# Gate chunk in three passes, late weight parts on VectorE, four tap sums on TensorE, mu in the first load, no table of shifts

## Chip, cores and metric

The kernel runs on one core of a Trainium2 chip. The metric is device time in microseconds (us). PE is TensorE's matmul engine and PEld its weight load, DVE is VectorE, ACT is ScalarE, POOL is GpSimd, SP is SyncE, which issues the kernel's DMAs.

## The reference

Three layers act on two batches of 4160 tokens with 192 channels, all in fp32.

```python
# 1: a convolution of 7 taps whose weights are a softmax per token and head (8 heads of 24 channels)
w = softmax(weight_gen, over the 7 taps)
x[b, s, h] = sum over k of w[b, s, k, h] * x_pad[b, s + k, h]
# 2: x_prev is x of the token before
xk = mu_k * x + (1 - mu_k) * x_prev
xr = mu_r * x + (1 - mu_r) * x_prev
x = sigmoid(xr @ w_r) * (relu(xk @ w_k) ** 2 @ w_v)       # 192 -> 1024 -> 192
# 3: h has 1024 channels, conv_w has 3 taps per channel
h = relu(x @ w_in)
x = (h * sigmoid(conv3(h, conv_w))) @ w_out
```

Each weight arrives as 64-bit floats; the kernel makes fp32 of it from two 32-bit words.

## The kernel before

Tokens are cut into 10 tiles (`SIZES`): two of 238, seven of 476 and one of 352 tokens, each for both batches. Channels stand on partitions: a 192-channel tensor is one block of 128 partitions and one of 64. To keep fp32 accuracy with fast fp32r matmuls, an operand is split into a high part and a low remainder, and a product is hi x hi, lo x hi and hi x lo. A 128-channel input takes three such passes; a 64-channel input has its high and its low part on the two halves of the partitions and takes two. So one product of 192 channels is five passes (`passes_in`, line 660).

Per tile the work is this. `attention` (530) does layer 1 with tokens on partitions, in 2, 4 or 3 slots of 128 tokens per batch. For a slot, `token` multiplies a window of 7 x 192 elements by the softmax weights into one of two `prod` buffers, and sums the 7 taps by three adds, all on POOL. For tile 0 alone the sum is made by seven fp32 matmuls with the identity (`total`) and copied out by ScalarE. `mixing` (574) transposes the sums on PE, mixes neighbouring tokens with mu and splits the result; the remainders are made on POOL, the 64-channel block is brought to its place by DMAs (`xB`). `moe1` (682) makes one chunk of 128 hidden channels of layer 2: five passes, relu, square, split, and five more passes into the accumulators `am` (128 channels) and `ar` (64 channels, high and low weight beside each other). There are 8 chunks. `gate_r` (664) makes the sigmoid gate in two chunks of five passes: channels 0 to 127, and channels 128 to 191, which stand twice in the weights (`wrA`, `wrB`, columns 128 to 255) so that the gate of the 64 channels lies on both halves of the partitions. `mix_out` (818) multiplies gate and accumulators and splits the product into `x2`; slice 3 of it holds the 64 channels' high part on the lower partitions and their remainder on the upper ones. `moe2` (854) is layer 3, again 8 chunks: five passes, relu, three taps, sigmoid, product, split (`c7` makes the high part on ScalarE; `c8` the remainder, on POOL from tile 7 on), five passes. `store` (913) adds the halves and writes out. Tiles 0 and 1 use the `_half` versions.

The weights come in 16 chunks (`prepare`, 478; the last of them are taken up between planner times 6 and 18: `w_in`, `w_out`, `conv_w`). `narrow` (399) makes fp32 of one: ScalarE scales the upper word, VectorE shifts and masks it and scales the lower word by the exponent, and PE adds the two in PSUM, with one fp32 matmul (identity) and one fp32r matmul. `split` (423) copies the high part on ScalarE, subtracts it on PE, and copies the remainder on ScalarE.

The order is made by a planner. Every step is put into `plan` with a time (`at`, 367), where one chunk is 1 and a tile 16, so tile i starts at 16 i. The steps become instructions, and `schedule` (168) is a list scheduler: with a cost per instruction (`cost`, 138) it picks, on the engine that is free first, the ready instruction with the lowest time. The order that results is issued as the program order of each engine's queue, SyncE's DMAs among them. `ORDER` (40) shifts the times of 393 of the 2983 plan items; its indices run from 11 to 1084, which are the loads, the softmax and tiles 0 to 4.

```python
    def at(t, fn, hold=0.0):
        plan.append((t + ORDER.get(len(plan), 0.0), len(plan), fn, hold))
```

Of the kernel before, what the change touches and what calls it, by code (L numbers as in the profile page):

```python
# [96 lines left out]
class Program:
# [986 lines left out]
```

## Time and profile before

| | |
|---|---|
| median of 3 runs | 736.1 us (734.06 to 736.75) |
| execution profiled | 739.15 us |
| its span, first to last instruction | 737.3 us |
| granted TensorE clock, mean | 0.989 of full |
| busy: PE, DVE, ACT, POOL | 706.5, 580.1, 646.6, 537.8 us |
| DMA | 44.58 MB, mean 60 GB/s |

Busy time is the union of an engine's instructions. A matmul's shown end is modelled and overlaps the next one, so what a pass costs in a run of passes is read from the length of the run, not from one pass. An idle stretch in brackets names what ended it.

### The profile page before, as it was taken

Reading aid. Unit: us, or ns where it says so; the run is one execution under the profiler, and the core shown is the slowest. Engines: PE = TensorE matmul, PEld = TensorE weight load, DVE = VectorE, ACT = ScalarE, POOL = GpSimd, SP = SyncE. Lnnn points to the kernel's source line nnn. Section 1 sums busy time; section 2 is a strip of 40 time slices with the busy share of each in tenths; the row PEclk is TensorE's granted clock in tenths of the full one; section 3 lists DMA queues with packets and bytes.
Section 4 is the critical chain, followed back from the end, with each engine's and each line's share of the span. In section 5 each row is a group of like instructions: output and inputs, shape, how many; then the busy total and the mean of one; then the engine's idle time right before and its main releaser. Section 6 shows DMA issues by size and latency. Waiting matters only on the chain.

```text
span 737.3 us, 10455 instructions
## 1 busy us (share of the span) xinstructions
PE 706.5 (96%) x3475; PEld 607.1 (82%) x3475; DVE 580.1 (79%) x959; ACT 646.6 (88%) x1340; POOL 537.8 (73%) x392
## 2 busy tenths in 40 slices
PE   4899988999999999999999999999999999999996
PEld 4687966888778888888888888888888888899995
DVE  5865968887998988787878787978796758686775
ACT  2788859999989999899989898989899989899986
POOL 1998997898999899999999999999022323242333
PEclk9899999999999999999999999999999999999999
DMA  8667112101211320231112202210002000200000
GB/s 271 196 198 228 56 54 54 39 35 59 68 39 55 88 75 1 73 80 48 54 58 57 87 1 69 74 48 1 21 15 59 1 20 7 55 0 21 1 21 29
DMA packets 18149, 44.58 MB, mean 60 GB/s; under 512 B 2864, under 2 KB 13616, under 8 KB 17968
## 3 DMA queue, kind: packets, MB, share of 16 engines
q1 hardware_dynamic: 18096, 43.93, 19.7%
q8 instruction: 27, 0.44, 0.3%
q14 instruction: 26, 0.21, 0.1%
HBM read 27.40 MB, written 6.39 MB: 46 GB/s over the span
## 4 chain that ended last, share of the span: by engine, by line
PE 80%; POOL 8%; ACT 6%; issue 3%; DVE 2%; DMA 1%; POOLq 0%; SPq 0%; ACTq 0%; DVEq 0%
PE pa L237 25%; PE pc L237 18%; PE bm L237 12%; PE am L237 11%; PE br L237 8%; PE ar L237 7%; POOL prod L237 5%; ACT pa L237 1%; DMA mu<-in_mu_dram 1%; ACT pc L237 1%; POOL s L237 1%; ACT L237 1%; DVE stage L237 1%; POOL xA L237 1%; POOL tok L237 0%
## 5 line engine op out<-in xcount | busy, mean ns | idle before, releaser
L237 DVE SCALAR_TENSOR_TENSOR pc<-h,cw,pc 128x476 f32<-128x476 f32 (+1 forms) x276 | 194.3, 705 | 40.4 <-ACT pc L237 37.4
L237 POOL TENSOR_TENSOR prod<-rows,sw 128x1344 f32<-128x1344 f32 x68 | 210.4, 3096 | 16.1 <-PE pa L237 15.2
L237 ACT ACTIVATE pa<-pa 128x476 f32<-128x476 f32 (+2 forms) x284 | 153.1, 540 | 31.7 <-PE pa L237 28.5
L237 POOL TENSOR_TENSOR prod<-prod 128x576 f32<-128x576 f32 (+1 forms) x132 | 161.5, 1223 | 9.3
L237 PE MATMUL bm<-g,wo 128*128 128x476 f32 (+1 forms) x411 | 133.1, 378 | 3.3 <-ACT g L237 2.8
L237 PE MATMUL am<-s,wv 128*128 128x476 f32 (+2 forms) x464 | 135.1, 359 | 0.0
L237 PE MATMUL pa<-xA,wkA 128*128 128x476 f32 (+2 forms) x450 | 117.6, 366 | 2.0 <-DVE s L237 1.5
L237 POOL TENSOR_TENSOR g<-stage,g 128x476 fp32r<-128x476 f32 (+1 forms) x41 | 47.5, 1158 | 97.5 <-ACT g L237 93.6
L237 PE MATMUL pc<-x,wiA 128*128 128x478 f32 (+1 forms) x414 | 113.2, 379 | 0.7 <-ACT x L237 0.6
L237 PE MATMUL ar<-s,wv 128*128 128x476 f32 (+2 forms) x336 | 106.5, 355 | 3.6 <-ACT s L237 3.6
L237 DVE TENSOR_TENSOR s<-pa,s 128x476 fp32r<-128x476 f32 (+1 forms) x139 | 88.1, 634 | 18.7 <-ACT s L237 18.2
L237 PE MATMUL br<-g,wo 128*128 128x476 f32 (+1 forms) x274 | 102.5, 375 | 0.0
L237 PEld LDWEIGHTS pa<-xA,wkA 128*128 128x128 f32 x450 | 79.7, 189 | 19.1 <-DVE s L237 5.5
L237 ACT ACTIVATE pc<-h,cw 128x476 f32<-128x476 f32 (+1 forms) x138 | 92.4, 670 | 1.2
L237 PEld LDWEIGHTS am<-s,wv 128*128 128x128 f32 x464 | 82.1, 189 | 11.2 <-ACT s L237 0.9
L237 DVE TENSOR_TENSOR pc<-h,pc 128x476 f32<-128x476 f32 x96 | 62.8, 654 | 33.7 <-ACT pc L237 33.5
L237 PEld LDWEIGHTS bm<-g,wo 128*128 128x128 f32 x411 | 75.9, 188 | 15.4 <-ACT g L237 4.3
L237 ACT ACTIVATE pc<-pc 128x476 f32<-128x476 f32 (+1 forms) x148 | 81.2, 548 | 8.2 <-DVE pc L237 6.5
L237 PEld LDWEIGHTS pc<-x,wiA 128*128 128x128 f32 x414 | 76.2, 190 | 12.7 <-DVE g L237 2.0
L237 ACT ACTIVATE h<-pc 128x478 f32<-128x478 f32 (+1 forms) x138 | 79.0, 573 | 8.4 <-PE pc L237 7.5
L237 PE MATMUL pa<-xB,wkB 128*128 128x476 f32 (+2 forms) x300 | 84.5, 361 | 0.6 <-DMA xB<-mk 0.6
L237 PE MATMUL pc<-x,wiB 128*128 128x478 f32 (+1 forms) x276 | 82.4, 377 | 0.0
(161 smaller groups left out, 1190.0 us busy)
## 6 DMA issues: line engine op xcount, KB each, us to landing
rows<-in_x_dram SPq DMA_DIRECT2D x14, 960.0 KB, 4.8
xB<-rm SPq DMA_DIRECT2D x28, 119.0 KB, 2.3
rows<-in_x_dram SPq DMA_DIRECT2D x4, 768.0 KB, 6.5
xB<-mk SPq DMA_DIRECT2D x16, 119.0 KB, 2.3
rows<-in_x_dram SPq DMA_DIRECT2D x2, 864.0 KB, 4.3
out_dram<-stage SPq DMA_DIRECT2D x7, 238.0 KB, 2.0
out_dram<-om SPq DMA_DIRECT2D x7, 238.0 KB, 2.0
stage<-in_moe_w_v_dram SPq DMA_DIRECT2D x4, 384.0 KB, 6.0
```

What stands on the lines that cost most here:

```text
L237: getattr(self.real[eng], method)(*a, **k)
```

## The change

The second gate chunk uses weights that have the high part in columns 128 to 191 and the low part in 192 to 255. Three passes give hi x and lo x on the two halves of the partitions; ScalarE copies the upper half down, VectorE adds it, and after the sigmoid a DMA copies the result to the upper half. Two DMAs (`swap`) put the low parts there after tiles 0 and 1, whose `gate_half` uses the old layout. `mix_out` makes its second copy of the 64 channels by a DMA in place of a ScalarE copy.

The weight chunks 8, 9, 10 and 12 to 15 (`w_in`, `w_out`) get mode 2: no matmul, and the remainder comes from a subtraction and an addition on VectorE. For slots 2 and 3 of both batches of tile 2, `total` sums the taps on PE. `mu` comes as four more columns of the first load of softmax weights. In the last batch of the last tile, POOL makes the high part of chunks 0 to 4 and VectorE the remainders of chunks 6 and 7, and the last two passes swap places. The last softmax load has a later time and hold, one of the softmax's additions goes from VectorE to ScalarE for the later tiles, the planner's price for a DMA out of SBUF goes from 0.45 to 0.58, and `ORDER` goes.

```diff
+HIGH = range(5)
+LOWS = {(NTILE - 1, NB - 1, k) for k in range(6, NF)}
+SUMS = {(2, 0, 2), (2, 0, 3), (2, 1, 2), (2, 1, 3)}
+MODES = [0, 0, 0, 0, 0, 0, 0, 0, 2, 2, 2, 0, 2, 2, 2, 2, 2]
-ORDER = {
...
         if method == "dma_start":
-            return 0.45, 0.0
+            return 0.58 if src == ["SBUF"] else 0.45, 0.0
...
     def at(t, fn, hold=0.0):
-        plan.append((t + ORDER.get(len(plan), 0.0), len(plan), fn, hold))
+        plan.append((t, len(plan), fn, hold))
...
     def narrow(st, n):
...
+        ACT.activation(px, f(hi), ACTF.Prelu, scale=2.0 ** -112, alpha=-(2.0 ** 32))
+        if mode[0] == 0:
...
         DVE.tensor_scalar(x, x, 3, None, op0=ALU.logical_shift_left)
         DVE.tensor_scalar(y, x, 0xFF800000, None, op0=ALU.bitwise_and)
+        zr = wz_r()[:, :n] if mode[0] == 1 else py
+        DVE.scalar_tensor_tensor(out=zr, in0=lo, scalar=2.0 ** -52, in1=py, op0=ALU.mult, op1=ALU.mult)
+        return Parts(px, wl_r()[:, :n], zr)
...
     def split(dst_hi, dst_lo, x):
+        if isinstance(x, Parts):
+            px, zl, zr = x.aps
+            ACT.copy(dst_hi, px)
...
+                DVE.tensor_tensor(zl, px, f(dst_hi), op=ALU.subtract)
+                DVE.tensor_tensor(dst_lo, zr, f(zl), op=ALU.add)
+            return
...
     def softmax_load(j, wg, t, hold=0.0):
-        w = sm[j][0]
+        w = both[:, (4 + KH * soft_at[j]) * (j > 0):4 + KH * soft_at[j + 1]]
...
         def s5():
-            DVE.tensor_scalar(z, z, 1e-9, None, op0=ALU.add)
+            if bank is None:
+                ACT.activation(z, z, ACTF.Copy, bias=1e-9)
...
-            if i < 1:
+            if i < 1 or (i, b, l) in SUMS:
                 def total():
...
                     for k in range(KS):
                         PE.matmul(z, lhsT=ident, rhs=y[:, k], start=(k == 0), stop=(k == KS - 1))
...
+                    if i:
+                        ACT.copy(x[:, l], z)
+                        return
...
     def gate_r(i, b, k, t):
         def go():
...
+            if k:
+                mm(p[:, :N], [(wrA[:, 0, 128:256], A[:, 0, :N]), (wrA[:, 0, 128:256], A[:, 1, :N]), (wrB[:, 0, 128:256], B[:, :N])])
+            else:
+                mm(p[:, :N], passes_in(wrA, wrB, A, B, slice(0, 128), N))
+        def fold():
+            a = attt_r()[0:64, :N]
+            ACT.copy(a, st["p"][64:128, :N])
+            DVE.tensor_tensor(st["p"][0:64, :N], st["p"][0:64, :N], a, op=ALU.add)
         def sg():
...
-            ACT.activation(r[:, :N], st["p"][:, :N], ACTF.Sigmoid)
+            ACT.activation(r[h, :N], st["p"][h, :N], ACTF.Sigmoid)
+            if k:
+                SP.dma_start(out=r[64:128, :N], in_=r[0:64, :N])
+        h = slice(0, 64 if k else 128)
         at(t, go)
+        if k:
+            at(t + 0.2, fold)
+        at(t + (0.6 if k else 0.3), sg)
...
         def a1():
-            ACT.copy(X[0:64, 3, c], r[0:64, :N])
             ACT.copy(X[:, 2, c], r[:, :N])
+            SP.dma_start(out=f(X[0:64, 3, c]), in_=f(X[0:64, 2, c]))
...
         def c7():
...
+            if (i, b) == (NTILE - 1, NB - 1) and fi in HIGH:
+                POOL.tensor_copy(g[:, 0, :N], st["q"][:, :N])
+            else:
+                ACT.copy(g[:, 0, :N], st["q"][:, :N])
         def c8():
...
-            (POOL if i >= ALONE else DVE).tensor_tensor(...)
+            (POOL if i >= ALONE and (i, b, fi) not in LOWS else DVE).tensor_tensor(...)
...
     def consts():
-        SP.dma_start(out=mu, in_=mus)
         DVE.tensor_scalar(onemu, mu, -1.0, 1.0, op0=ALU.mult, op1=ALU.add)
...
-    softmax_load(3, wg_rest[:, (slots[1] + slots[2]) * KH:], 18.2, 50.0)
+    softmax_load(3, wg_rest[:, (slots[1] + slots[2]) * KH:], 20.5, 60.0)
...
+    def swap():
+        for W in (wrA, wrB):
+            SP.dma_start(out=f(W[:, 0, DM:256]), in_=f(W[:, 1, 128:DM]))
+    at(30.5, swap)
```

## Rows read from the trace of the kernel before

**Rows 1.** Windows: length; busy us (count) of PE, PEld, DVE, ACT, POOL; clock; DMA

```profile
0.00:60.00 60.00, 46.36 (x247) 38.04 (x248) 41.66 (x83) 39.34 (x103) 39.92 (x34) 0.94 0.71 219
60.00:120.00 60.00, 50.92 (x325) 43.41 (x324) 45.82 (x75) 46.02 (x101) 53.28 (x40) 0.97 0.34 106
280.00:700.00 420.00, 419.91 (x2004) 364.04 (x2003) 328.07 (x527) 384.74 (x780) 282.95 (x205) 1.00 0.13 37
700.00:737.30 37.30, 31.16 (x176) 28.12 (x174) 25.45 (x50) 28.39 (x67) 13.33 (x15) 0.97 0.08 25
```

**Rows 2.** Chain of waits in order of time, 10 to 125: start us, us, what

```profile
66.05 3.01 POOL prod L237
69.13 1.43 POOL prod L237
...
70.62 1.03 POOL prod L237
71.71 0.59 POOL tok L237
...
105.16 2.38 POOL xA L237 x2
```

**Rows 3.** Windows of PE alone: busy us (instructions), clock, DMA share, GB/s

```profile
90.00:95.00 5.00, 3.01 (x23) 1.00 0.01 3
95.00:100.00 5.00, 4.83 (x24) 0.66 0.01 2
110.00:115.00 5.00, 3.70 (x23) 1.00 0.08 18
115.00:120.00 5.00, 2.82 (x13) 1.00 0.79 177
120.00:125.00 5.00, 5.00 (x20) 0.66 0.00 0
```

**Rows 4.** Chain of waits, runs of passes of 476 and of 352 columns

```profile
445.05 1.08 PE pc L237 x5
...
691.47 1.62 PE pa L237 x10
```

**Rows 5.** Timeline around tile 5's mix_out: start us, us, engine, operation, out<-in

```profile
388.36 0.57 ACT L237 CAST x<-ar 64x476 fp32r<-64x476 f32 x1
...
390.32 0.65 DVE L237 TENSOR_TENSOR x<-ar,x 64x476 fp32r<-64x476 f32 x1
...
392.25 0.59 PE L237 MATMUL pc<-x,wiB 128*128 128x478 f32 x2
```

**Rows 6.** DMA issues: count, KB each, median us from issue to landing

```profile
xB<-rm SPq DMA_DIRECT2D x28, 119.0 KB, 2.3
```

**Rows 7.** Waits of SyncE's queue: us in total, times, longest us

```profile
SPq L237 <- POOL prod L237: 199.4, 16, 27.2
```

**Rows 8.** Groups of PE by form, 46.5 to 82: busy us, mean ns | idle before

```profile
L237 PE MATMUL bm<-stage,ident 128*128 128x512 f32 x4 | 2.0, 593 | 0.0
...
L237 PE MATMUL bm<-stage,ident 128*128 128x384 f32 x4 | 1.6, 485 | 0.0
```

**Rows 9.** Timeline of the start, 0 to 24

```profile
0.73 0.20 POOL L237 MEMSET ident<- 128x128 f32 x1 [0.29 <-POOLq L1073]
...
1.01 0.29 POOL L237 TENSOR_SCALAR_AFFINE_SELECT ident<-ident 128x128 f32<-128x128 f32 x1
...
8.43 0.17 DVE L237 TENSOR_SCALAR onemu<-mu 128x4 f32<-128x4 f32 x1 [2.58 <-DMA mu<-in_mu_dram]
8.51 3.03 DVE L237 TENSOR_TENSOR prod<-rows,sw 128x1344 f32<-128x1344 f32 x2
...
20.33 2.51 PE L237 MATMUL pc<-prod,ident 128*128 128x192 f32 x14 [0.61 <-DVE am L237]
```

**Rows 10.** Groups by form, 700 to 737.3

```profile
L237 POOL TENSOR_TENSOR g<-stage,g 128x354 fp32r<-128x354 f32 x8 | 7.6, 950 | 15.3 <-ACT g L237 15.3
...
L237 ACT CAST g<-stage 128x354 fp32r<-128x354 f32 x7 | 3.4, 483 | 0.9 <-DVE stage L237 0.9
```

More of the change, by code (lines that the diff above doesn't have):

```diff
@@ L38 @@
 SPARE = 20
-ORDER = {
[49 rows of a table removed]
-}
 def f(ap):
@@ L251, in conv_moe_kernel @@
 @with_exitstack
-def conv_moe_kernel(ctx: ExitStack, tc: tile.TileContext, xp, wg_first, wg_rest, mus, w_k, w_v, w_r, w_in, conv_w, w_out, out):
+def conv_moe_kernel(ctx: ExitStack, tc: tile.TileContext, xp, wg_first, wg_rest, w_k, w_v, w_r, w_in, conv_w, w_out, out):
     nc = tc.nc
@@ L285, in __call__ @@
             return self.tiles[(self.n - 1) % len(self.tiles)]
-    mu = new("mu", [128, 4])
     onemu = new("onemu", [128, 4])
@@ L311, in conv_moe_kernel @@
     wz_r = Ring([t.rearrange("p a b -> p (a b)") for t in g_r.tiles[:2]])
+    wl_r = Ring([t.rearrange("p a b -> p (a b)") for t in g_r.tiles[2:]])
     rows_r = ring("rows", 2, [128, max(SLOTS) + PAD, DM])
@@ L328, in conv_moe_kernel @@
     KH = KS * NH
-    sw = new("sw", [128, sum(slots), KS, NH])
+    both = new("sw", [128, 4 + sum(slots) * KH])
+    mu = both[:, 0:4]
+    sw = both[:, 4:].rearrange("p (s k h) -> p s k h", k=KS, h=NH)
     sm = []
@@ L367, in at @@
     def at(t, fn, hold=0.0):
-        plan.append((t + ORDER.get(len(plan), 0.0), len(plan), fn, hold))
+        plan.append((t, len(plan), fn, hold))
+    serial = [1 << 20]
     def later(t, fn):
-        heapq.heappush(plan, (t, (1 << 20) + prog.item, fn, 0.0))
+        serial[0] += 1
+        heapq.heappush(plan, (t, serial[0], fn, 0.0))
     def mm(dst, passes):
@@ L395, in fetch, with __init__, rearrange, __getitem__ @@
         return st
-    on_pe = [False]
+    mode = [0]
+    class Parts:
+        def __init__(self, *aps):
+            self.aps = aps
+        def rearrange(self, *a, **k):
+            return Parts(*(x.rearrange(*a, **k) for x in self.aps))
+        def __getitem__(self, c):
+            return Parts(*(x[c] for x in self.aps))
     def narrow(st, n):
@@ L414, in narrow @@
             return px
-        ACT.activation(px, f(hi), ACTF.Copy, scale=2.0 ** -112)
         DVE.tensor_scalar(x, x, 3, None, op0=ALU.logical_shift_left)
-        DVE.scalar_tensor_tensor(out=x, in0=hi, scalar=0x80000000, in1=x, op0=ALU.bitwise_and, op1=ALU.bitwise_or)
         DVE.tensor_scalar(y, x, 0xFF800000, None, op0=ALU.bitwise_and)
-        DVE.scalar_tensor_tensor(out=f(z), in0=lo, scalar=2.0 ** -52, in1=py, op0=ALU.mult, op1=ALU.mult)
-        DVE.tensor_tensor(px, px, f(z), op=ALU.add)
-        return px
+        zr = wz_r()[:, :n] if mode[0] == 1 else py
+        DVE.scalar_tensor_tensor(out=zr, in0=lo, scalar=2.0 ** -52, in1=py, op0=ALU.mult, op1=ALU.mult)
+        return Parts(px, wl_r()[:, :n], zr)
     def split(dst_hi, dst_lo, x):
+        if isinstance(x, Parts):
+            px, zl, zr = x.aps
+            ACT.copy(dst_hi, px)
+            if mode[0] == 1:
+                DVE.tensor_tensor(zl, px, f(dst_hi), op=ALU.subtract)
+                PE.matmul(px, lhsT=signs[:, 0:128], rhs=zl, start=True, stop=False, skip_group_check=True)
+                PE.matmul(px, lhsT=signs[:, 0:128], rhs=zr, start=False, stop=True, skip_group_check=True)
+                ACT.copy(dst_lo, px)
+            else:
+                DVE.tensor_tensor(zl, px, f(dst_hi), op=ALU.subtract)
+                DVE.tensor_tensor(dst_lo, zr, f(zl), op=ALU.add)
+            return
         ACT.copy(dst_hi, x)
-        if on_pe[0] and prog.space(x) == "PSUM":
+        if prog.space(x) == "PSUM":
             PE.matmul(x, lhsT=signs[:, 128:256], rhs=dst_hi, start=False, stop=True, skip_group_check=True)
@@ L486, in use @@
             def use(st=st, n=n, go=go, j=j):
-                on_pe[0] = j < 16
+                mode[0] = MODES[j]
                 go(narrow(st[0], n))
@@ L495, in softmax_load @@
     def softmax_load(j, wg, t, hold=0.0):
-        w = sm[j][0]
-        at(t, lambda: SP.dma_start(out=w.rearrange("p s k h -> p (s k h)"), in_=wg), hold)
+        w = both[:, (4 + KH * soft_at[j]) * (j > 0):4 + KH * soft_at[j + 1]]
+        at(t, lambda: SP.dma_start(out=w, in_=wg), hold)
     def softmax(j, a, b, eng, times, bank):
@@ L515, in s5 @@
         def s5():
-            DVE.tensor_scalar(z, z, 1e-9, None, op0=ALU.add)
+            if bank is None:
+                ACT.activation(z, z, ACTF.Copy, bias=1e-9)
+            else:
+                DVE.tensor_scalar(z, z, 1e-9, None, op0=ALU.add)
             DVE.reciprocal(m, z)
@@ L670, in go @@
             st["p"] = p
-            sl = slice(128 * k, 128 * k + 128)
-            mm(p[:, :N], passes_in(wrA, wrB, xin[i, b, 1, 0], xin[i, b, 1, 1], sl, N))
+            A, B = xin[i, b, 1, 0], xin[i, b, 1, 1]
+            if k:
+                mm(p[:, :N], [(wrA[:, 0, 128:256], A[:, 0, :N]), (wrA[:, 0, 128:256], A[:, 1, :N]), (wrB[:, 0, 128:256], B[:, :N])])
+            else:
+                mm(p[:, :N], passes_in(wrA, wrB, A, B, slice(0, 128), N))
[3 more added lines that the diff above has]
+            DVE.tensor_tensor(st["p"][0:64, :N], st["p"][0:64, :N], a, op=ALU.add)
         def sg():
@@ L795, in mix_out_half, with out_passes @@
         at(t + 0.4, d2)
-    def out_passes(W, fi, s, n, am, ar, one=False):
+    def out_passes(W, fi, s, n, am, ar, one=False, back=False):
         s0, s1 = s[:, 0, :n], s[:, 1, :n]
@@ L802, in out_passes @@
         PE.matmul(ar[:, :n], lhsT=W[:, fi, 2], rhs=s0, start=a and not one, stop=False, skip_group_check=one)
-        PE.matmul(am[:, :n], lhsT=W[:, fi, 0], rhs=s1, start=False, stop=z, skip_group_check=one)
-        PE.matmul(ar[:, :n], lhsT=W[:, fi, 2], rhs=s1, start=False, stop=z, skip_group_check=one)
+        for p, k in ((ar, 2), (am, 0)) if back else ((am, 0), (ar, 2)):
+            PE.matmul(p[:, :n], lhsT=W[:, fi, k], rhs=s1, start=False, stop=z, skip_group_check=one)
     def carry(i, b, t):
@@ L889, in c7 @@
             st["g"] = g
-            ACT.copy(g[:, 0, :N], st["q"][:, :N])
+            if (i, b) == (NTILE - 1, NB - 1) and fi in HIGH:
+                POOL.tensor_copy(g[:, 0, :N], st["q"][:, :N])
+            else:
+                ACT.copy(g[:, 0, :N], st["q"][:, :N])
         def c8():
             g = st["g"]
-            (POOL if i >= ALONE else DVE).tensor_tensor(g[:, 1, :N], st["q"][:, :N], f(g[:, 0, :N]), op=ALU.subtract)
+            (POOL if i >= ALONE and (i, b, fi) not in LOWS else DVE).tensor_tensor(g[:, 1, :N], st["q"][:, :N], f(g[:, 0, :N]), op=ALU.subtract)
         def go2():
@@ L899, in go2 @@
                 acc2["r"] = br_r()
-            out_passes(wo, fi, st["g"], N, acc2["m"], acc2["r"])
+            out_passes(wo, fi, st["g"], N, acc2["m"], acc2["r"], back=last and b == NB - 1 and fi == NF - 1)
         at(t + 0.5, go)
@@ L1015, in conv_moe_kernel @@
     while plan:
-        t, n, fn, hold = heapq.heappop(plan)
-        prog.now, prog.hold, prog.item = t, hold, n
+        t, _, fn, hold = heapq.heappop(plan)
+        prog.now, prog.hold = t, hold
         fn()
@@ L1020, in conv_moe_kernel @@
         prog.schedule()
-_ARGS = ("x", "first", "rest", "mu", "moe_w_k", "moe_w_v", "moe_w_r", "moe2_w_in", "moe2_conv_w", "moe2_w_out")
+_ARGS = ("x", "first", "rest", "moe_w_k", "moe_w_v", "moe_w_r", "moe2_w_in", "moe2_conv_w", "moe2_w_out")
 def _layout(inputs):
@@ L1048, in _layout @@
     w = np.asarray(inputs["weight_gen"]).transpose(0, 1, 3, 2)
+    mu = np.stack([c for k in "kr" for m in [rows(inputs["moe_mu_" + k]).reshape(DM)]
+                   for c in (m[:128], np.concatenate([m[128:], m[128:]]))], axis=1)
     a = {
         "x": np.concatenate([np.zeros_like(x[:, :PAD]), x], axis=1),
-        "first": chunks(w, 0, 1),
+        "first": np.concatenate([mu, chunks(w, 0, 1)], axis=1),
         "rest": chunks(w, 1, NTILE),
-        "mu": np.stack([c for k in "kr" for m in [rows(inputs["moe_mu_" + k]).reshape(DM)]
-                        for c in (m[:128], np.concatenate([m[128:], m[128:]]))], axis=1),
         "moe_w_k": rows(inputs["moe_w_k"]),
```

3 lines of the change are left out of this document (removed), and 49 rows, old and new, of the table ORDER.

## The prediction

> **What bounds the kernel now.** I first read the busy time of each engine in a few long stretches [rows 1]. From 280 to 700 us TensorE (PE) has no idle time (419.91 of 420.00), so there every pass removed is time removed. From 60 to 120 us it has 9.1 us idle (50.92 of 60.00) while GpSimd (POOL) is busy for 53.28. So the kernel has a front that something other than PE sets, a long middle that PE sets, and a tail with 37.30 - 31.16 = 6.1 us of idle PE.
>
> The chain of waits says what sets the front [rows 2]: from 66 to 105.16 it runs almost without a break through POOL's window sums. One slot of a window sum is a product of 3.01 us, then adds of 1.43, 1.03 and 0.59 us. These are tile 2's eight slots, one behind another. At 105.16 POOL turns to tile 2's mixing, and only then can TensorE have tile 2. The fine stretches show it [rows 3]: in 110:120 PE is busy for 3.70 and 2.82 of 5.00 us, in 120:125 for all of it. I take 120 us as the moment from which PE is full.
>
> The execution profiled took 739.15 us (span 737.3), 3.05 above the median of 736.1. I sum changes against the execution and carry them to the median.
>
> **Part by part.**
>
> *Gate.* Five back-to-back passes of 476 columns take 1.08 us [rows 4], 0.216 each; ten of tile 9's 352 columns take 1.62, 0.162 each. Two passes go in each of 16 second chunks (8 tiles, 2 batches): 28 x 0.216 + 4 x 0.162 = 6.7 us, all in the full middle. Added per chunk are a 64-partition ScalarE copy, a VectorE add and a transfer. `mix_out` gives up a 64-partition ScalarE copy (0.57 us [rows 5]) for a transfer, so ScalarE is even; VectorE gets 0.65 us more, 10 us over the kernel, and has room: 328.07 of 420.00 busy [rows 1]. The bank of PSUM is held about a microsecond longer, covered by the second bank. Lower bound of the gain 4 us, if the longer bank hold costs PE 0.17 us a chunk; I take 6.7, since PE has no idle time that could hide a saving.
>
> *The two transfers per chunk.* A 119 KB copy within SBUF lands 2.3 us after issue [rows 6]. For the gate's r there are four units of the planner's clock (each some 20 passes or 4.3 us long) until it is read. For the input of the second layer it is tight. Now the 64-partition copy starts at 388.36, the 128-partition one follows, and TensorE reads the last slice in the second of the passes at 392.25, that is at 392.46 [rows 5]. Afterwards the 128-partition copy can have the first place (388.36 to 388.93), and its transfer lands at about 391.2. That is 1.2 us early: I cost it at nothing. What covers it is SyncE's queue being free at that moment; if it isn't, the loss is a wait of PE (first rival).
>
> *Weight chunks.* Seven late chunks (three of 512 columns, four of 384) lose on PE an fp32 pass that the trace shows as two records and passes of fp32r. For 512 columns two records take 1.0 us together and 0.59 singly, so the second starts about 0.41 after the first and each holds PE for that long [rows 8]; with two passes of 0.23 (0.216 scaled to 512) that is 1.3 us a chunk. For 384: 0.8 less 0.485, so 0.32 each, and 0.35 for the rest: 1.0. Sum 8 us of PE. ScalarE loses a copy per chunk, some 0.5 us; VectorE goes from three operations to five, about 1.3 us a chunk, 9 us. VectorE is busy for 45.82 of 60.00 us there [rows 1]. None of this is on POOL's chain, so I book no gain of its own: it makes room for the next part.
>
> *Tap sums.* Four of tile 2's eight slots lose their three adds: 4 x (1.43 + 1.03 + 0.59 + 0.06 of starting) = 12.4 us off the chain [rows 2]. PE gets four sets of seven fp32 products. One set, 14 records, took 2.51 us in tile 0 [rows 9], so 10 us on PE, which the 8 us above and the 9 us of idle time between 60 and 120 us hold. The last slot now ends by PE and a ScalarE copy (2.5 + 0.4 us) in place of its 3.1 us of adds, so tile 2's sums are whole not at 105.2 but at about 105.2 - 12.4 + 2.9 = 95.7. PE is full 9.5 us earlier. Not all of that is gained: the passes that PE did between 110 and 120 (23 and 13 of them [rows 3]) are left over and cost at most 36 x 0.216 = 7.8 us at full rate, about 5 since many have 238 columns. Gain 4.5 us; 9.5 if tile 1's second layer also moves up, 0 if the next wait behind POOL (the chain of `mixing`, ScalarE's table loads) ends as late as now.
>
> *mu.* VectorE now waits for mu until 8.43 before it starts the first products at 8.51 [rows 9]. The rows that the products read were issued before mu; bounds 0 (they land as late) and 2.6 (VectorE's whole idle time before that row); they share the queue, so I take 0.3. POOL's first products wait for this, so it moves the front.
>
> *Tail.* The last batch's g goes in five chunks from ScalarE to POOL, two remainders from POOL to VectorE, and the last two passes swap. A cast is 0.48 us on ScalarE, a remainder 0.95 on POOL [rows 10]; on VectorE a like one takes 0.65 for 476 columns [rows 5], so about 0.5 here. Handed over, 5 x 0.48 = 2.4 us leave ScalarE. The last remainder ends 0.4 us sooner, and the 64-channel output can begin one pass (0.16) sooner. A POOL copy of 354 columns isn't in the trace; between 0.48 and 0.95 I take 0.7, as it has one input. `mix_out`'s transfer costs up to 1.2 us where the last chunk starts at once. Net -1; ends -2.5 and +1.2.
>
> *No table.* The shifts belong to plan items 11 to 1084 of 2983, hence to tiles 0 to 4. What they gave cannot be seen in one trace. Bounds: a gain of 2, and a loss of 10 us, about what PE idles between 60 and 120 us once more. I take a loss of 3: POOL's queue sets the front and has hardly an idle moment in which order could matter. The moved load (18.2 to 20.5), the reciprocal's addition on ScalarE and the planner's dearer transfer I cost at nothing; they lie beside POOL's chain.
>
> *Sum:* -6.7 - 4.5 - 0.3 - 1 + 3 = -9.5, so 729.6 for a profiled execution and 726.6 for the median. I say **727**.
>
> **The clock.** In 95:100 and 120:125 the mean granted clock was 0.66 [rows 3], so part of those five microseconds ran at 1.2 and not at 2.4 GHz, after 90:95 and 115:120 with PE busy for only 3.01 and 2.82. Each costs 5 x 0.34 = 1.7 us. My sum leaves both in. The Trainium skill (TensorE: Matmul & The Clock Gate, Part 1) has the clock throttled by default and released by activity; by that, tap sums that fill these gaps would give back 3.4 us and the sum would be 723.2. The trace agrees so far as both drops stand behind idle stretches.
>
> **The rivals.**
> 1. *SyncE's queue holds the new transfers* (slower). It is in order, and it already stands 199.4 us waiting for POOL's products, up to 27.2 at a time [rows 7]. If such a load stands ahead of an x transfer when POOL runs late, PE waits for every microsecond beyond the 1.2 of slack. That decides at 16 places: 2.3 us late on average costs about 1 us each, 16 in all: 743. Against it: the list scheduler takes a transfer only when it thinks it ready, and its price for a copy is now 0.58. Chance 0.12.
> 2. *The front comes back*: without the table the start and tile 1 lose about what the tap sums give, 8 us instead of 3, and tile 2 is no earlier (4.5). For it: PE has 60.00 - 46.36 = 13.6 us idle already in the first 60 us [rows 1], where the shifts are dense; against it stands POOL's chain. 727 + 5 + 4.5 = 736.5, within the noise. Chance 0.13.
> 3. *PE's saving doesn't arrive*, as ScalarE (384.74 of 420.00) sets the middle once PE is shorter. Then only front and tail count: 727 + 6.7 = 733.7. Against it: ScalarE's work stays even. Chance 0.04.
> 4. *The front gains all*: PE is full 9.5 us earlier with tile 1 done (5 us more) and no half-clock stretch stands behind it (3.4 more): 718. Chance 0.17.
> 5. *POOL's first copy is slow.* It is an operation that POOL has not run before the tail. POOL's first select started 0.08 us after the memset in front of it [rows 9], which speaks against a cost of first use. If there is one, what exceeds the idle time that POOL has between two chunks of the tail is late at the end; a delay of the size of one product (3.01 us) or two gives 729 to 732. The Trainium skill (GPSIMD Engine Reference, section 2.1) gives about 6 us for the first call of freshly loaded code, with no row in the profile; no run here shows that this copy is such a call. Chance 0.03.
>
> **How the numbers follow.** Half a per cent, 3.7 us, is about what a measurement can tell here: faster is below 732.4, slower above 739.8. The forecast (720 to 732.4) has 0.51; with rivals 4 and 5, faster is 0.71, rivals 2 and 3 give 0.17 for no change, rival 1 gives 0.12 for slower. The range runs from 715, which takes in rival 4 and the better ends of the tail, to 740, which takes in rivals 2, 3 and 5 and leaves out most of rival 1.
>
> **What the changed profile would show.** Gate: runs of three and five wr passes, 32 fewer in all. Front: POOL's tile 2 products 3 us apart in pairs, its first mixing of tile 2 near 93, PE full from about 110. Weights: no fp32 pair on the late chunks, five VectorE operations each. Tail: POOL writes g twice in five chunks; PE idles under 5 us after 700. I am wrong if PE between 130 and 700 us waits for DMA on x or r, if PE is full no earlier than 118, or if the 16 gates save less than 5 us of PE.

## The result and the profile after

The changed kernel takes **726.88 us** (median of 4 runs, 726.37 to 727.82). The kernel before takes 736.15 beside it (4 runs, 734.06 to 736.75). The ratio, taken over all runs of both and not over the two medians, is 0.988, with a 95% interval of 0.9859 to 0.9902: 8.8 us less, give or take 1.6. The forecast was 727. The execution profiled took 727.82 us with a span of 726.0.

Busy time and the chain of waits, from the page of the changed kernel (`L189` is its helper's line, as `L237` was before):

```profile
PE 697.7 (96%) x3467; PEld 603.5 (83%) x3467; DVE 588.7 (81%) x992; ACT 644.3 (89%) x1335; POOL 525.6 (72%) x383
...
PE 82%; ACT 8%; DVE 7%; issue 2%; DMA 1%; SPq 0%; DVEq 0%; ACTq 0%
```

The same chain in the kernel before:

```profile
PE 80%; POOL 8%; ACT 6%; issue 3%; DVE 2%; DMA 1%; POOLq 0%; SPq 0%; ACTq 0%; DVEq 0%
```

POOL no longer has a share in the chain that ends last, though it is still busy for 525.6 us. The long stretches that answer to [rows 1] (length, then busy us and count of PE, PEld, DVE, ACT, POOL, then clock, DMA share, GB/s):

```profile
0.00:60.00 60.00, 45.25 (x246) 39.17 (x247) 46.66 (x96) 40.11 (x105) 40.19 (x35) 0.91 0.72 226
60.00:120.00 60.00, 53.89 (x362) 48.46 (x361) 46.99 (x85) 46.97 (x98) 55.99 (x37) 1.00 0.30 100
280.00:700.00 420.00, 420.00 (x2018) 364.81 (x2017) 336.44 (x546) 389.90 (x792) 273.94 (x201) 1.00 0.16 45
700.00:726.00 26.00, 20.26 (x116) 18.42 (x114) 19.68 (x40) 18.48 (x43) 11.63 (x15) 0.97 0.09 25
```

The middle is as full as it was. The front looks better: PE is busy for 53.89 us between 60 and 120, not 50.92. PE alone in five-microsecond stretches, beside [rows 3]:

```profile
90.00:95.00 5.00, 3.68 (x22) 1.00 0.29 111
95.00:100.00 5.00, 5.00 (x34) 1.00 0.23 89
105.00:110.00 5.00, 3.90 (x30) 1.00 0.53 123
110.00:115.00 5.00, 4.83 (x29) 1.00 0.38 85
115.00:120.00 5.00, 5.00 (x27) 1.00 0.00 0
120.00:125.00 5.00, 5.00 (x25) 1.00 0.01 3
```

PE is full from about 110, ten microseconds sooner, and neither 95:100 nor 120:125 has a lowered clock any more. Taken alone, these rows say that the front gained some ten microseconds. The experiments say that it gained almost nothing that lasted.

A second measure keeps one from reading the front by its busy share alone: POOL's mixing of `stage` with `xA`, 16 instructions of 476 columns from tile 2 to tile 8, the last of full width, always at the same places of the program. The row gives their shortest, median and longest ns, and the start of the first and of the last. The kernel before:

```profile
L237 POOL TENSOR_TENSOR xA<-stage,xA x16: 1206/1216/1228, 105.2 to 584.2; 128x476 fp32r<-128x476 f32 x16
```

The changed kernel:

```profile
L189 POOL TENSOR_TENSOR xA<-stage,xA x16: 1203/1218/1232, 101.6 to 575.2; 128x476 fp32r<-128x476 f32 x16
```

In the traces of runs 7 to 10, whose front is nearly the same, it begins at 101.0 to 102.1 and at 574.7 to 575.7, so differences of about a microsecond tell nothing.

So of the 11.3 us by which the profiled span is shorter (737.3 - 726.0), 3.6 are there at tile 2, 9.0 at tile 8's mixing, and the last 2.3 come behind it (153.1 us from that mixing to the end, now 150.8), where the gates of tiles 8 and 9 lie as well as the tail.

### The profile page after: what moved, and what is told of

It is laid out like the page before. It is cut to its first block, busy times and chain, and to the rows that moved or that the text cites. A ratio compares the mean times of both kernels' runs of the same rounds, so it can differ in the third digit from the quotient of the medians.

```text
span 726.0 us, 10500 instructions
## 1 busy us (share of the span) xinstructions
PE 697.7 (96%) x3467; PEld 603.5 (83%) x3467; DVE 588.7 (81%) x992; ACT 644.3 (89%) x1335; POOL 525.6 (72%) x383
## 4 chain that ended last, share of the span: by engine, by line
PE 82%; ACT 8%; DVE 7%; issue 2%; DMA 1%; SPq 0%; DVEq 0%; ACTq 0%
PE pa L189 25%; PE pc L189 19%; PE bm L189 12%; PE am L189 11%; PE br L189 7%; PE ar L189 7%; DVE stage L189 2%; DVE pc L189 2%; ACT pa L189 2%; ACT pc L189 1%; DMA rows<-in_x_dram 1%; ACT att L189 1%; ACT h L189 1%; ACT s L189 1%; DVE g L189 1%
## 5 line engine op out<-in xcount | busy, mean ns | idle before, releaser
L189 POOL TENSOR_TENSOR prod<-rows,sw 128x1344 f32<-128x1344 f32 x68 | 210.1, 3092 | 15.1 <-PE pa L189 14.1
L189 DVE SCALAR_TENSOR_TENSOR pc<-h,cw,pc 128x476 f32<-128x476 f32 (+1 forms) x276 | 194.1, 705 | 32.0 <-ACT pc L189 28.9
L189 ACT ACTIVATE pa<-pa 128x476 f32<-128x476 f32 (+2 forms) x286 | 154.6, 542 | 26.4 <-PE pa L189 21.3
L189 POOL TENSOR_TENSOR prod<-prod 128x576 f32<-128x576 f32 x124 | 151.9, 1225 | 8.4
L189 PE MATMUL bm<-g,wo 128*128 128x476 f32 (+1 forms) x411 | 134.9, 377 | 1.3 <-ACT g L189 1.3
L189 PE MATMUL am<-s,wv 128*128 128x476 f32 (+2 forms) x464 | 133.2, 359 | 1.9 <-ACT s L189 1.5
L189 PE MATMUL pa<-xA,wkA 128*128 128x476 f32 (+2 forms) x456 | 117.3, 362 | 1.6 <-ACT rm L189 0.6
L189 POOL TENSOR_TENSOR g<-stage,g 128x476 fp32r<-128x476 f32 (+1 forms) x41 | 47.5, 1159 | 96.8 <-ACT g L189 86.6
L189 PE MATMUL pc<-x,wiA 128*128 128x478 f32 (+1 forms) x414 | 113.2, 377 | 0.3 <-ACT x L189 0.3
L189 PE MATMUL ar<-s,wv 128*128 128x476 f32 (+2 forms) x336 | 106.0, 356 | 2.5 <-DVE s L189 1.5
L189 DVE TENSOR_TENSOR s<-pa,s 128x476 fp32r<-128x476 f32 (+1 forms) x140 | 88.9, 635 | 17.1 <-ACT s L189 16.0
L189 PE MATMUL br<-g,wo 128*128 128x476 f32 (+1 forms) x274 | 102.7, 375 | 0.0
L189 PEld LDWEIGHTS pa<-xA,wkA 128*128 128x128 f32 x456 | 79.9, 189 | 17.7 <-DVE s L189 2.6
L189 PEld LDWEIGHTS am<-s,wv 128*128 128x128 f32 x464 | 80.8, 188 | 15.5 <-DVE x L189 2.7
L189 ACT ACTIVATE pc<-h,cw 128x476 f32<-128x476 f32 (+1 forms) x138 | 92.5, 670 | 1.2
L189 ACT ACTIVATE pc<-pc 128x476 f32<-128x476 f32 (+1 forms) x146 | 80.2, 549 | 11.2 <-DVE pc L189 6.4
L189 ACT ACTIVATE h<-pc 128x478 f32<-128x478 f32 (+1 forms) x138 | 79.1, 573 | 9.4 <-PE pc L189 9.1
L189 PEld LDWEIGHTS bm<-g,wo 128*128 128x128 f32 x411 | 76.7, 188 | 12.1 <-ACT g L189 1.6
L189 PEld LDWEIGHTS pc<-x,wiA 128*128 128x128 f32 x414 | 75.4, 188 | 12.8 <-DVE g L189 2.3
L189 PE MATMUL pa<-xB,wkB 128*128 128x476 f32 (+2 forms) x304 | 84.5, 357 | 0.0
L189 DVE TENSOR_TENSOR pc<-h,pc 128x476 f32<-128x476 f32 x96 | 62.8, 654 | 26.1 <-ACT pc L189 25.8
L189 PE MATMUL pc<-x,wiB 128*128 128x478 f32 (+1 forms) x276 | 81.5, 376 | 0.0
```

The costliest lines, as they stand in the source:

```text
L189: getattr(self.real[eng], method)(*a, **k)
```

## The experiments

Each kernel was timed against the kernel before on the same chip (medians there 736.95 for runs 1, 4, 5 and 11, 736.13 for 2, 7, 8 and 9, 736.73 for 3, 6, 10 and 12). Parts are compared by these ratios, taken over all runs: a difference of 0.001 is 0.74 us, and the half-width of a difference is the root of the sum of both half-widths squared.

**1. The tap sums back on POOL.**

```diff
-SUMS = {(2, 0, 2), (2, 0, 3), (2, 1, 2), (2, 1, 3)}
+SUMS = set()
```

> The changed kernel with tile 2's four tap sums back on POOL. POOL theory: 12.4 us come back on POOL's chain, tile 2's sums are whole 9 to 10 us later, PE is full near 120 and not near 110, and after the 10 us of fp32 passes that go and the work that can be done meanwhile the kernel takes 4.5 us more, 731.4 (729 to 736). Rival (the front is set by ScalarE and VectorE, PE only gets 10 us of passes less): within 1.5 us of 726.9 or faster, PE full no later than 112.

Measured: 727.85 us, ratio 0.9886 (0.9867 to 0.9905). Against the changed kernel's 0.988 the four sums on PE bring 0.4 us, give or take 2.1. The 4.5 us forecast for them are excluded. Neither expectation held whole: the time is the rival's, the moment from which PE is full is the POOL theory's. With the sums, PE is full some ten microseconds sooner, as the forecast wanted. PE's stretches without the sums:

```profile
105.00:110.00 5.00, 2.83 (x16) 1.00 0.07 28
110.00:115.00 5.00, 3.57 (x22) 1.00 0.48 112
115.00:120.00 5.00, 4.22 (x17) 0.67 0.36 83
120.00:125.00 5.00, 4.16 (x20) 0.99 0.00 0
```

Here PE is not full even in 120:125, and a half-clock stretch is back. What ate the gain is in PE's groups from 20 to 125 us (busy us, mean ns, idle before). The products with `ident`, in the changed kernel:

```profile
L189 PE MATMUL pa<-prod,ident 128*128 128x192 f32 x51 | 9.1, 329 | 0.2 <-POOL prod L189 0.2
L189 PE MATMUL pc<-prod,ident 128*128 128x192 f32 x28 | 4.9, 326 | 0.0
```

and without the sums:

```profile
L189 PE MATMUL pc<-prod,ident 128*128 128x192 f32 x14 | 2.4, 326 | 0.0
L189 PE MATMUL pa<-prod,ident 128*128 128x192 f32 x7 | 1.3, 326 | 0.0
```

The sums cost PE 14.0 - 3.7 = 10.3 us. From 0 to 200 us PE alone shows, in the changed kernel:

```profile
0.00:200.00 200.00, 177.47 (x966) 0.97 0.38 119
```

and without the sums:

```profile
0.00:200.00 200.00, 170.61 (x908) 0.96 0.38 119
```

That is 6.9 us less idle time. The half-clock stretch of 115:120 (0.67 for 1.00) is 1.7 us more: some 9 us gained for 10.3 us of added passes. The mixing row closes the account:

```profile
L189 POOL TENSOR_TENSOR xA<-stage,xA x16: 1181/1221/1239, 104.7 to 575.2; 128x476 fp32r<-128x476 f32 x16
```

Tile 2 is mixed 3.1 us later without the sums, and tile 8 at the same 575.2. PE fills its idle time with the sums themselves, and not with passes that it would else do later; the passes that were to move up stay behind.

Nor did tile 2's mixing follow POOL. The changed kernel's POOL from 86 to 104 us (start, us, operation; in brackets the idle time before it and what ended it):

```profile
86.49 6.07 POOL L189 TENSOR_TENSOR prod<-rows,sw 128x1344 f32<-128x1344 f32 x2
92.51 5.54 POOL L189 TENSOR_TENSOR sw<-sw,stage 128x448 f32<-128x448 f32 x5
99.39 1.16 POOL L189 TENSOR_TENSOR sw<-sw,stage 128x448 f32<-128x448 f32 x1 [1.34 <-DVE stage L189]
101.57 2.39 POOL L189 TENSOR_TENSOR xA<-stage,xA 128x476 fp32r<-128x476 f32 x2 [1.02 <-PE pa L189]
```

POOL's products end at 92.56, in pairs as forecast. Then POOL multiplies softmax weights of a later tile, waits for VectorE, and last for an input of the mixing. The view names PE for this last wait, whose transposes of another unit end at that moment. But by the kernel the two subtractions read what VectorE made from the first transposes and what ScalarE cast from it, and the first cast runs from 100.90 to 101.49. The chain of the mixing, from the timeline of the changed kernel:

```profile
94.48 2.44 PE L189 MATMUL pa<-prod,ident 128*128 128x192 f32 x14
96.76 0.60 PE L189 MATMUL pa<-ident,tok 128*128 128x128 f32 x4
...
97.39 0.56 ACT L189 COPY stage<-pa 128x476 f32<-128x476 f32 x1
...
99.22 1.24 DVE L189 SCALAR_TENSOR_TENSOR stage<-stage,onemu,pa 128x476 f32<-128x476 f32 x2
...
100.90 0.59 ACT L189 CAST xA<-stage 128x476 fp32r<-128x476 f32 x1
```

The last sum ends at 96.9, and the first transposes (`ident`, `tok`) come right behind it in PE's order. They read only the first batch's sums, whose last copy ScalarE made at 78.49. Without the sums on PE they come 15 us sooner, and the cast with them:

```profile
81.65 0.60 PE L189 MATMUL pa<-ident,tok 128*128 128x128 f32 x4
...
87.42 0.59 ACT L189 CAST xA<-stage 128x476 fp32r<-128x476 f32 x1
```

There the mixing waits for POOL's own queue alone, until 104.7. So the sums freed POOL and at the same time put the start of the mixing behind themselves on PE: the wait on POOL became a wait on PE's queue and the chain of `mixing` behind it.

**2. The weight chunks' remainders back on PE.**

```diff
-MODES = [0, 0, 0, 0, 0, 0, 0, 0, 2, 2, 2, 0, 2, 2, 2, 2, 2]
+MODES = [0] * 17
```

> The changed kernel with all weight chunks in the old way (fp32 pass and remainders on PE, second copy on ScalarE). The forecast booked nothing for this part: with 8 us of PE and about 4 us of ScalarE back and 9 us of VectorE gone, under 1.5 us more than the changed kernel's 726.9 (ratio to the kernel before 0.988 to 0.990). New theory, since the tap sums alone brought nothing although PE is full 11 us earlier with them: every pass that the front must do counts in full, so 8 us of passes cost 4 to 8 us, ratio 0.993 to 0.999.

Measured: 726.88 us, ratio 0.9875 (0.9859 to 0.989): no difference (-0.4, give or take 1.9). The forecast of no gain held, and the new theory of 4 to 8 us fell. The work is there: in the first 200 us PE is busy for 183.80 us, not 177.47, 6.3 us more where the estimate was 8. It is hidden, but by idle and half-clock time of PE, not by room for the sums. From 50 to 55 us PE is idle in the changed kernel where the work was. Two stretches of the changed kernel, PE alone:

```profile
50.00:55.00 5.00, 2.47 (x13) 0.70 0.84 207
55.00:60.00 5.00, 5.00 (x30) 0.61 0.52 127
```

and with the weights on PE:

```profile
50.00:55.00 5.00, 3.84 (x28) 1.00 0.91 228
55.00:60.00 5.00, 4.91 (x37) 1.00 0.75 165
```

**3. Both off together.** If the freed PE time and the sums only work together, each alone is worth nothing, but the pair is worth something.

```diff
-MODES = [0, 0, 0, 0, 0, 0, 0, 0, 2, 2, 2, 0, 2, 2, 2, 2, 2]
+MODES = [0] * 17
-SUMS = {(2, 0, 2), (2, 0, 3), (2, 1, 2), (2, 1, 3)}
+SUMS = set()
```

> The changed kernel with both front parts undone: tile 2's tap sums back on POOL and all weight chunks the old way. Singly each of them cost nothing that can be told (ratios 0.9886 and 0.9875 against 0.988). If they are independent, nothing again: 0.988 (0.9865 to 0.9895). If either one does what the other does (each takes about 10 us off a front in which PE's passes and POOL's chain add up), undoing both costs 4 us and more: 0.993 and up, with PE full at 120 us or later.

Measured: 728.71 us, ratio 0.9881 (0.986 to 0.9902): 0.1 us from the changed kernel's ratio, give or take 2.2. All four combinations lie between 0.9875 and 0.9886. The two parts do nothing that can be measured, alone or together.

**4. The gate in five passes again.** The second chunk of the gate in 5 passes, without the fold, r's transfer and the two swaps; all else as changed.

```diff
-            if k:
-                mm(p[:, :N], [(wrA[:, 0, 128:256], A[:, 0, :N]), (wrA[:, 0, 128:256], A[:, 1, :N]), (wrB[:, 0, 128:256], B[:, :N])])
-            else:
-                mm(p[:, :N], passes_in(wrA, wrB, A, B, slice(0, 128), N))
+            mm(p[:, :N], passes_in(wrA, wrB, A, B, slice(128 * k, 128 * k + 128), N))
...
-        if k:
-            at(t + 0.2, fold)
-        at(t + (0.6 if k else 0.3), sg)
+        at(t + 0.3, sg)
...
-    at(30.5, swap)
```

> The changed kernel with the second gate chunk in five passes again (no fold, no transfer of r, no swap of weights), all else as changed. PE theory: 32 passes come back in the full stretch, 28 x 0.216 + 4 x 0.162 = 6.7 us, so about 733.6 us against 726.9 of the changed kernel, and PE has no idle time from 280 to 690 us in either. ScalarE theory (ScalarE sets the middle once PE is shorter): the passes cost under 2 us, at most 729.

Measured: 731.22 us, ratio 0.9934 (0.9917 to 0.9951). The three passes are worth 4.0 us in the changed kernel, give or take 2.0, between the two theories (6.7, and under 2). The mixing row, and two stretches of all engines:

```profile
L189 POOL TENSOR_TENSOR xA<-stage,xA x16: 1199/1216/1222, 101.7 to 578.2; 128x476 fp32r<-128x476 f32 x16
```

```profile
280.00:680.00 400.00, 400.00 (x1900) 346.59 (x1899) 312.76 (x504) 362.56 (x728) 266.08 (x193) 1.00 0.15 43
160.00:200.00 40.00, 39.30 (x185) 33.06 (x184) 36.28 (x61) 37.76 (x76) 27.97 (x20) 1.00 0.15 38
```

The front is the same (101.7 for 101.6), and the difference grows along the middle: 3.0 us at tile 8's mixing, 4.3 in the span. The same stretches of the changed kernel:

```profile
280.00:680.00 400.00, 400.00 (x1901) 345.50 (x1900) 323.25 (x522) 372.39 (x752) 268.10 (x195) 1.00 0.16 46
160.00:200.00 40.00, 38.33 (x177) 31.39 (x176) 36.61 (x62) 37.94 (x76) 28.13 (x20) 1.00 0.16 40
```

PE is full in the middle either way. VectorE and ScalarE are busy for some 10 us more each in these 400; over the whole kernel it is 7.7 and 4.4 (588.7 for 581.0, 644.3 for 639.9). PE's busy time falls by 5.7 us over the whole kernel (703.4 to 697.7). From 160 to 200 us PE is busy for 1 us less with three passes than with five and waits for ScalarE's `s` (1.5 us, 0.4 with five), so not all of the saving arrives there.

**5 and 6. The kernel before without its table, and then with the new gate alone.** Two experiments, the second on top of the first:

```diff
-        plan.append((t + ORDER.get(len(plan), 0.0), len(plan), fn, hold))
+        plan.append((t, len(plan), fn, hold))
```

> The kernel before with the table of shifts taken away and nothing else. Theory (POOL's queue sets the front and has little to order): 3 us more than before, about 739; bounds 734 to 746. Rival (the table had been what held the front together): 744 and more, with PE's idle time before 120 us up by 8 or more. Other rival (worth nothing): 736.

```diff
+            if k:
+                mm(p[:, :N], [(wrA[:, 0, 128:256], A[:, 0, :N]), (wrA[:, 0, 128:256], A[:, 1, :N]), (wrB[:, 0, 128:256], B[:, :N])])
+            else:
+                mm(p[:, :N], passes_in(wrA, wrB, A, B, slice(0, 128), N))
...
+        if k:
+            at(t + 0.2, fold)
+        at(t + (0.6 if k else 0.3), sg)
...
+    at(30.5, swap)
```

> The kernel before without its table (1.0031 of the kernel before with it), with the gate's second chunk in three passes and nothing else of the change; ScalarE has the fold's 16 copies on top. PE theory: 6.7 us less than without it, 731.7, ratio 0.994. As measured in the changed kernel: 4.3 us less, 0.9973. ScalarE theory: under 2.5 us less, 1.000 and up.

Measured: without the table 738.45 us (12 runs), ratio 1.0031 (1.0015 to 1.0046): the table is worth 2.3 us, give or take 1.1. With the gate in three passes on top, 732.05 us (6 runs), ratio 0.9929 (0.9901 to 0.9957): 7.5 us less, give or take 2.4. Both came out as their first theories had it (739 and 731.7). The mixing rows, without the table:

```profile
L237 POOL TENSOR_TENSOR xA<-stage,xA x16: 1199/1215/1222, 105.3 to 585.7; 128x476 fp32r<-128x476 f32 x16
```

and with the gate on top:

```profile
L237 POOL TENSOR_TENSOR xA<-stage,xA x16: 1206/1220/1237, 105.6 to 577.5; 128x476 fp32r<-128x476 f32 x16
```

With the gate alone tile 2 is mixed no sooner, and tile 8 8.2 us sooner (577.5 for 585.7; the two executions profiled are 9.6 us apart, the medians 6.4). The gate's saving needs nothing of the front.

**7. The old tail.**

```diff
-HIGH = range(5)
-LOWS = {(NTILE - 1, NB - 1, k) for k in range(6, NF)}
+HIGH = range(0)
+LOWS = set()
...
-            out_passes(wo, fi, st["g"], N, acc2["m"], acc2["r"], back=last and b == NB - 1 and fi == NF - 1)
+            out_passes(wo, fi, st["g"], N, acc2["m"], acc2["r"])
```

> The changed kernel with the last batch's high parts on ScalarE, all its remainders on POOL and the old order of the last two passes. Forecast: the tail's share, 1 us more (2.5 less 1.2 for the transfer stays out of this), so 728, ratio about 0.9895. Rival (a gain of 3 or more in the tail carries the surplus that the gate and the sums did not bring): 730 and more, with PE's idle time after the last full stretch up by 2 us. Rival of the first copy's cost: 726 or less.

Measured: 729.1 us, ratio 0.9909 (0.9892 to 0.9925). The tail's part is worth 2.1 us, give or take 2.0, and 1.0 in the spans profiled (727.0 and 726.0), between the forecast and its rival. POOL's groups in the changed kernel from 690 to 726 us:

```profile
L189 POOL TENSOR_TENSOR g<-stage,g 128x354 fp32r<-128x354 f32 x8 | 7.6, 954 | 11.2 <-ACT g L189 10.9
...
L189 POOL CAST g<-stage 128x354 fp32r<-128x354 f32 x4 | 1.9, 482 | 0.4 <-DVE stage L189 0.3
```

POOL copies 354 columns in 482 ns, as fast as ScalarE [rows 10]. The first of its five copies stands in a row of its own, 478 ns at 709.63, 0.14 us behind the VectorE product that it reads (708.97 and 0.52), so it is no slower than the others.

**8. The copy for the second layer back on ScalarE**, in place of the transfer:

```diff
+            ACT.copy(X[0:64, 3, c], r[0:64, :N])
             ACT.copy(X[:, 2, c], r[:, :N])
-            SP.dma_start(out=f(X[0:64, 3, c]), in_=f(X[0:64, 2, c]))
```

> The changed kernel with the second copy of the 64 channels in mix_out made by ScalarE again, no transfer of x. Forecast: the transfer is hidden and ScalarE does not set the middle, so within 1 us of 726.9 (ratio 0.987 to 0.990). ScalarE theory (the gate brought only 4 of 6.7 us because ScalarE is nearly full): 16 x 0.57 = 9 us more of ScalarE cost 2 us and more, ratio 0.991 and up. Transfer theory (the transfer makes PE wait): faster, ratio under 0.986.

Measured: 727.57 us, ratio 0.988 (0.9861 to 0.99), the changed kernel's own. Neither the transfer nor the copy is on the path. Its middle, all engines:

```profile
280.00:680.00 400.00, 399.93 (x1898) 344.05 (x1897) 322.42 (x521) 375.42 (x761) 266.87 (x194) 1.00 0.15 43
```

SyncE's queue in the changed kernel, with both transfers in it, beside [rows 7]:

```profile
SPq L189 <- POOL prod L189: 112.9, 14, 18.4
```

**9. `mu` by a load of its own**, as before:

```diff
-        w = both[:, (4 + KH * soft_at[j]) * (j > 0):4 + KH * soft_at[j + 1]]
+        w = both[:, 4 + KH * soft_at[j]:4 + KH * soft_at[j + 1]]
...
+        SP.dma_start(out=mu, in_=wg_first[:, 0:4])
...
-    softmax_load(0, wg_first, -100.2)
+    softmax_load(0, wg_first[:, 4:], -100.2)
```

> The changed kernel with mu in a load of its own behind the first rows, as before. Forecast: 0.3 us more; not to be told from 726.9 (ratio 0.987 to 0.990), VectorE's first product near 8.5 us. Rival (the load of mu held the start up by more): 1 us and more, with everything in the front later by as much.

Measured: 727.11 us, ratio 0.988 (0.9864 to 0.9895): no difference. The start of the changed kernel:

```profile
2.81 0.17 DVE L189 TENSOR_SCALAR onemu<-sw 128x4 f32<-128x4 f32 x1 [1.91 <-DMA sw<-in_first_dram]
7.27 3.03 DVE L189 TENSOR_TENSOR prod<-rows,sw 128x1344 f32<-128x1344 f32 x2 [1.35 <-DMA rows<-in_x_dram]
8.98 7.50 PE L189 MATMUL pa<-prod,ident 128*128 128x192 f32 x28 [8.98 <-DVE prod L189]
```

and with `mu` loaded by itself:

```profile
7.53 0.17 DVE L189 TENSOR_SCALAR onemu<-sw 128x4 f32<-128x4 f32 x1 [1.58 <-DMA sw<-in_first_dram]
7.62 3.03 DVE L189 TENSOR_TENSOR prod<-rows,sw 128x1344 f32<-128x1344 f32 x2
9.32 6.28 PE L189 MATMUL pa<-prod,ident 128*128 128x192 f32 x28 [9.32 <-DVE prod L189]
```

VectorE's first products start 0.35 us later with a load for `mu`, but PE is through with the sums of them sooner (9.32 + 6.28 = 15.60, not 16.48). An earlier start is not an earlier end.

**10. The planner's small pieces as before**: the price of a transfer, the last softmax load's time and hold, and the addition back on VectorE.

```diff
-            return 0.58 if src == ["SBUF"] else 0.45, 0.0
+            return 0.45, 0.0
...
-            if bank is None:
-                ACT.activation(z, z, ACTF.Copy, bias=1e-9)
-            else:
-                DVE.tensor_scalar(z, z, 1e-9, None, op0=ALU.add)
+            DVE.tensor_scalar(z, z, 1e-9, None, op0=ALU.add)
...
-    softmax_load(3, wg_rest[:, (slots[1] + slots[2]) * KH:], 20.5, 60.0)
+    softmax_load(3, wg_rest[:, (slots[1] + slots[2]) * KH:], 18.2, 50.0)
```

> The changed kernel with the small planner pieces undone: the price of 0.45 for every transfer, the last softmax load at 18.2 and held to 50 us, the softmax's addition on VectorE. Forecast: they cost and bring nothing, 0.988 (0.9865 to 0.9895). Rival (the 5 us that the parts undone singly do not account for come from the order that these pieces set): 0.992 and up, with more idle time of PE before 130 us.

Measured: 727.35 us, ratio 0.9865 (0.9846 to 0.9884): nothing (-1.1, give or take 2.1).

**11. The changed kernel with the table of before.** The shifts were carried to the items that answer to those of before; the new items get none.

```diff
+    index = [0]
...
-    def at(t, fn, hold=0.0):
-        plan.append((t, len(plan), fn, hold))
+    def at(t, fn, hold=0.0, extra=0):
+        key = index[0] - 1 if extra == 2 else None if extra else index[0]
+        index[0] += extra == 0
+        plan.append((t + ORDER.get(key, 0.0), len(plan), fn, hold))
```

> The changed kernel with the old table of shifts, each shift on the plan item that it belonged to (the gate's fold takes its chunk's shift, the swap none). If the table's worth is independent of the other parts: 3 us less, about 724. If the shifts fitted only the front that POOL set: no gain, 726.9 to 732, with new idle time of PE before 130 us.

Measured: 724.59 us (5 runs), ratio 0.9849 (0.9828 to 0.9871), the fastest of all, 2.3 us below the changed kernel's ratio, give or take 2.2. Its mixing row:

```profile
L241 POOL TENSOR_TENSOR xA<-stage,xA x16: 1202/1218/1232, 98.0 to 570.5; 128x476 fp32r<-128x476 f32 x16
```

Tile 2 is 3.6 us earlier than in the changed kernel, and here, where no passes were added, the lead is still there at tile 8 (570.5 for 575.2). That is what a gain in the front looks like when it lasts. (The execution profiled, 723.38, is the fastest of its five, so the trace shows more than the 2.3.)

**12. The same with the weights on PE.** Both as in 2 and 11:

> The changed kernel with the old table of shifts (0.9849) and all weight chunks the old way (0.9875 alone). If the two are independent: 0.9845. If the clock stays up in 40 to 60 us, as it did with the weights on PE, and the table packs the front: 0.982 and under, the fastest so far. If the table's order needs the freed PE: 0.988 and up.

Measured: 726.88 us, ratio 0.9864 (0.9847 to 0.988), 1.1 us above the run before, give or take 2.0, at none of the three values expected. Whether the table needs the weight chunks off PE stays open.

## Why the prediction was right, point by point

The total and the direction were right, and two of its three larger terms within their noise; **one term failed**, and others made up for it.

- **Gate (-6.7): right alone, too large beside the other parts.** The second chunk has 3 passes, 8 per tile and batch where there were 10. Undone in the changed kernel it costs 4.0 us (2.0 to 6.0), put alone into the kernel before it brings 7.5 (5.1 to 9.9); the forecast lies in the second interval and 0.7 above the first. The lower bound of 4 was for PSUM held longer. The runs show no such wait: the 1 us of PE's idle time between 160 and 200 us ends with ScalarE's `s`. "ScalarE is even" held: 4.4 us more by the fold (run 4), 5.9 less by the transfer in `mix_out` (run 8).
- **Transfers and ScalarE (0): right.** PE waits for no DMA of x or r, and its middle is full. The slower rival, SyncE's queue, did not come: the queue now waits 112.9 us for POOL's products, 18.4 at the longest, less than in [rows 7]. The rival that ScalarE sets the middle falls by run 8, where ScalarE does 3 us more in 400 (5.9 in all) and the time is the same.
- **Weight chunks (0): right in size, wrong in the reason.** "It makes room for the next part" was not what happened: the next part brings nothing with the room or without it (runs 1 to 3). PE's share was 5.0 us by the whole kernel's busy time (702.7 for 697.7) and 6.3 by the first 200 us, not 8.
- **Tap sums (-4.5): wrong.** The step that failed is "10 us on PE, which the 8 us above and the 9 us of idle time between 60 and 120 us hold". I used the same idle time twice: once to hide the sums' passes, and once as the gain from an earlier full PE. Once PE is full, every pass that was added is a pass left over, so the account is idle time removed less work added, 9 less 10.3. "PE full from about 110" was right (110.4 in place of about 120) and proved nothing. Tile 2's mixing was forecast near 93 and came at 101.6; the text's own end, "0 if the next wait behind POOL (the chain of `mixing`, ScalarE's table loads) ends as late as now", is close to what happened: it ended 3.6 us sooner, and the wait was the chain of `mixing`, whose start the sums themselves had moved on PE from 81.65 to 96.76. I gave it as a bound and not as the value, since I read POOL as the only thing that held tile 2.
- **`mu` (-0.3): right.** VectorE's products start 1.24 us sooner than in [rows 9], 0.35 of it by the missing load (run 9), and nothing of it can be measured in the time.
- **Tail (-1): right.** 2.1, give or take 2.0, and 1.0 by the spans. POOL's copy took 0.48 and not 0.7 us. The rival of a slow first copy falls: it starts 0.14 us behind its input and takes 0.48. The Trainium skill (GPSIMD Engine Reference, section 2.1) has the first call of freshly loaded code at about 6 us; no row here shows such a delay for this copy. PE's idle time after 700 us was to be under 5 and is 26.00 - 20.26 = 5.74; the output behind the last pass (721.59 to 726.0) makes up most of it, which the bound overlooked.
- **No table (+3): right.** It is 2.3 in the kernel before and 2.3 in the changed one. The rival in which the whole front comes back got its cost wrong and half of its claim right: the front's gain is missing, but not because of the table.
- **The clock.** Both half-clock stretches that the prediction names went (95:100 and 120:125 now have 1.00). The Trainium skill (TensorE: Matmul & The Clock Gate, Part 1) has activity release the throttle; the rows agree as far as PE idles less in front of them (busy for 3.68 us in 90:95, not 3.01, and 5.00 in 115:120, not 2.82). A third one, which the prediction doesn't name, was in the kernel before at 30:40 (0.65 and 0.66), and 30:35 still has 0.66. Another came: 50:60 has 0.70 and 0.61 with PE idle in front, where the weight chunks' passes had been. No gain can be traced to it: run 2 has the better clock and the same time. The rival in which the front gains all and the clock's 3.4 us come on top did not come either.

Put together, runs 5, 6 and 3 lie on a path from the kernel before to the changed one, and each step has a measure. The table away is +2.3 (run 5), the gate then -7.5 (run 6), then everything but sums and weight chunks -3.5, give or take 2.6 (0.9929 to 0.9881, runs 6 and 3), and sums and weight chunks together -0.1 (run 3). By construction these steps add up to the whole -8.8, so no part of the change is without a measure. Undone singly, the parts of the third step come to -1.0 (tail -2.1, planner +1.1, the rest 0), which lies within the noise of -3.5. Open is why the gate is worth 7.5 alone and 4.0 in the changed kernel, 3.5 apart, give or take 3.1: it may lose part of its worth beside the others, or the two may differ by noise.

Without the failed term the forecast's sum would have been -5.0; run 1, which is the change without that term, measured -8.4, give or take 1.4. So the exact hit is partly luck: what the sums did not bring, the other terms brought above their estimates (gate alone 7.5 for 6.7, tail 2.1 for 1, the table's loss 2.3 for 3), none of them by more than its noise.

## What to carry to other kernels

When work is moved onto the engine that will be the bound, the gain is the idle time that disappears less the work that is added; an earlier moment from which that engine is full is no gain by itself. Look also at what the moved work is queued in front of: here it held back the transposes that it was meant to hasten. Follow one instruction that comes in tile after tile: a lead that shrinks on the way was borrowed, and one that stays is real. Passes taken out of a stretch in which the engine never idles come off the time (here 4.0 to 7.5 us measured for 6.7 counted), and such a part can be tried alone.
